# Moving PSUM copies, turns and a value product in the first batch of a fused attention and MLP kernel

## The chip, the cores and the metric

The kernel runs on one core of a Trainium2 chip. A core has a matrix engine (TensorE, in the profile PE, with its weight loads as PEld), a vector engine (VectorE, DVE), a scalar engine (ScalarE, ACT), a general engine (GpSimd, POOL) and an engine that only issues transfers (SyncE, SP). Each has its own queue of instructions, and they are tied together by semaphores. TensorE writes into PSUM; DVE and ACT copy from there into SBUF, the working memory.

The metric is the device time of one launch in microseconds (us), smaller is better. Of several runs the median is given. A profile is one more execution, recorded instruction by instruction; "span" is the time from its first to its last instruction.

## The reference

Two things are computed one after the other: an attention in which scores far below a row's maximum are dropped, and a two-layer MLP with an exact GELU. Cut to what matters:

```python
batch, n_heads, seq, head_dim = (8, 8, 576, 64)
scores = q @ k^T / sqrt(head_dim)
thresh = max(scores, axis=-1) - tau
scores = where(scores >= thresh, scores, -1e9)
attn   = exp(scores - max(scores)); attn /= sum(attn) + 1e-9
x = (attn @ v) transposed and reshaped to (4608, 512)
h = x @ w_in                      # 512 x 2048
g = 0.5 * h * (1 + erf(h / sqrt(2)))
out = g @ w_out                   # 2048 x 512
```

All inputs and the result are float32; the weights w_in and w_out arrive in a wider type and are converted in the kernel.

## The kernel before, in words

**Tiles.** Two heads are handled as a pair p (32 pairs; 4 of them make one batch element). A pair's 576 query rows are cut into five chunks i: four of 128 and a last one (i == NC, NC = 4) that holds the 64 remaining rows of both heads. One chunk of one pair is a "slot" n. The loop over slots (L1130) writes out, slot by slot, what every engine does; the order in which an engine gets its instructions is the order of these calls. Nothing is scheduled behind the program's back (`manual_schedule`).

**A slot.** `scores` (L392) multiplies q and k on PE into two PSUM tiles `sc` of two banks each (one tile for the last chunk); there are only two such tiles in all. `softmax_head` (L404) takes row maxima on DVE (L413), thresholds on POOL (L416) and exp on ACT (L418). `softmax_tail` (L421) applies the threshold and sums on DVE (L434), and only then are the score banks free for the next slot.

**The first batch.** The first four pairs (`EARLY`, slots 0 to 19, `BATCH` = 20) are worked in two rounds: chunks 0 and 1 of all four pairs (slots 0 to 7), then chunks 2, 3 and 4 (slots 8 to 19). Their probabilities p are turned by TensorE: `turn_p_early` (L337) turns 128x128 pieces into PSUM tiles named `tr`, and copies them into `pT` (L354, L363 for a full chunk; L358, L367 for the last one, on ACT, but on DVE for the last pair). A slot's turns are called in the next slot. `weigh_v` (L557) multiplies v with pT on PE (L572) into one PSUM tile `xT` and copies x^T into `xall` (L582, ACT). The tiles `tr`, `xT`, `hT`, `o_ps` and `idle` share four PSUM banks (tag "mm"). From slot 20 on (pairs 4 to 31) p is turned on DVE instead (L533) and regrouped by transfers that SP issues (L555).

**Which x^T when.** A list `due` holds what the next slot shall weigh. The second part of a pair's rows (columns TOK = 256 to S = 576) is entered one slot after the pair's last chunk has been turned: the x^T of pairs 0, 1, 2 is weighed in slots 12, 15, 18 and that of pair 3 in slot 21.

**Conversions.** The weights come as 64-bit words. `convert_first` (L188) does two ACT instructions (L199, L200) for a piece, `convert_second` (L203) two on DVE (L207, L208), and `add_low_bits` one on POOL (L219) a slot later. In slots 12, 15 and 18, before x^T is weighed, `convert_ahead` puts several pieces' ACT parts into ACT's queue.

**The MLP.** `fill` (L688) puts matmuls of the MLP between a slot's scores and the next: first layer hT (L664), second layer o_ps (L679). How many is set by `goal`, a table of how much should be done by slot n; `owed` is what is still to be put in. In the first batch the first layer of block 0 is done and its results are held without GELU (L631); in slot 20, `gelus_held` (L641) applies the eight GELUs in one go, between two loads of ACT's function table. Slot 20 puts in no MLP work; slot 21 puts in a share of 0.4 of what is owed, and slot 22 the rest.

**Keeping TensorE busy.** `keep_busy` (L292) puts dummy matmuls of the identity matrix into the queue at the end of the slots that `BUSY` (L1123) lists; slot 20 has eight.

Of the kernel before, what the change touches and what calls it, by code (L numbers as in the profile page):

```python
# [18 lines left out]
def kernel(  # L19
# [28 lines left out]
    nc = tc.nc  # L48
    ctx.enter_context(tc.manual_schedule())

    B, H, S, D = q.shape
    d_model, d_ff = moe_w_in.shape
    P = 128
    Q = 32
    HP = H // 2
    NP = B * HP
    EARLY = HP
    NC = S // P
    MAIN = NC * P
    TAIL = S - MAIN  # L60
# [5 lines left out]
    TOK = 256  # L66
# [89 lines left out]
    LATER = 2  # L156
# [65 lines left out]
    def convert_ahead(steps):  # L222

        while raws and len(ahead) <= steps:
            convert_first()
# [111 lines left out]
    def turn_p_early(p, i):  # L337


        s = st[p]  # L340
        if i == 0 or (p < HP and i == 2):
            s["pT"] = [one.tile([P, KR, S], FP32, tag=f"pT{e}", name=f"pT{e}") for e in range(2)]
        w = s.pop(("p", i))
        n = 1 if i == NC else 2

        def turn(to, at):
            nc.tensor.transpose(to, w[:, at:at + P], ident)  # L347

        for e in range(n):
            tr = ps.tile([P, NC, P], FP32, tag="mm", name="tr")  # L350
            for c in range(NC):
                turn(tr[:, c, :], e * (S + TAIL) + c * P)
            if i < NC:
                nc.scalar.copy(s["pT"][e][:, 0:NC, i * P:(i + 1) * P], tr)  # L354
        if i == NC:
            copy = nc.vector.tensor_copy if p == EARLY - 1 else nc.scalar.copy
            for e in range(2):
                copy(s["pT"][e][:, 0:NC, MAIN:S], tr[:, :, e * TAIL:(e + 1) * TAIL])  # L358
        tails = s["pT"][0][:, NC, :]
        tr = ps.tile([P, NC, P], FP32, tag="mm", name="tr")  # L360
        turn(tr[:, 0, :], MAIN if i < NC else S - P)
        if i < NC:
            nc.scalar.copy(tails[:, i * P:(i + 1) * P], tr[:, 0, :])  # L363
            return
        for e in range(2):
            rows = slice(e * TAIL, (e + 1) * TAIL)
            copy(tails[rows, MAIN:S], tr[P - TAIL:P, 0, rows])  # L367

    def scale_q(p):
        t = st[p]["q"]  # L370
# [183 lines left out]
            for e in (1, 0):  # L554
                nc.sync.dma_start(by_64(s["pT"][e])[:, 2 * a + h, :, :], turned_p[rows, e, h, :, :])  # L555

    def weigh_v(p, lo, hi):  # L557


        b, hp = divmod(p, HP)  # L560
        s = st[p]
        xT = ps.tile([P, 512], FP32, tag="mm", name="xT")
        for c in range(KR):
            for e in range(2):
                f = slice(e * D, (e + 1) * D)
                to = xT[f, 0:hi - lo]
                if p < EARLY:
                    rhs = s["pT"][0 if c == NC else e][:, c, lo:hi]
                else:
                    to = to.rearrange("p (g s) -> p g s", s=2 * Q)  # L570
                    rhs = by_64(s["pT"][e])[:, lo // (2 * Q):hi // (2 * Q), c, :]
                nc.tensor.matmul(  # L572
                    to, lhsT=s["v"][:, e, c, :], rhs=rhs, start=(c == 0), stop=(c == KR - 1))
        for n, o, at, size in in_blocks(b, lo, hi):
            if n not in x_blk:
                x_at[n] = x_slot(x_place(n))
                x_blk[n] = xall[:, x_at[n], :, :]
            to, x = x_blk[n][:, hp, o:o + size], xT[:, at - lo:at - lo + size]
            if p < EARLY and size == TOK:
                to = to.rearrange("q (p c) -> q c p", c=2)  # L580
                x = x.rearrange("q (c p) -> q c p", c=2)
            nc.scalar.copy(to, x)  # L582

    def weigh_half(p, c):

# [14 lines left out]
    def in_blocks(b, lo, hi):  # L600
        while lo < hi:
            n, o = divmod(b * S + lo, TOK)
            size = min(TOK - o, hi - lo)
            yield n, o, lo, size
            lo += size
# [495 lines left out]
    BATCH = HP * SLOTS  # L1101
# [3 lines left out]
    START = 2 * HP + 2  # L1105
# [14 lines left out]
    HALVED = (2, 3)  # L1120
    DIVIDE_LATE = {14: 0, 16: 1, 19: 2, 22: 3}
    STEPS = [0, 1, 1, 1, 1, 1, 2, 1, 2, 2, 2, 2, 3, 2, 2, 3, 2, 2, 2]
    BUSY = {1: 2, 6: 2, 8: 2, BATCH: 4}  # L1123

    tokens = 0
    owed = 0.0
    due = []
    leaving = []
    loads = iter(())
    for n in range(len(slots) + WEIGH + 1):  # L1130
        p, i = slots[n] if n < len(slots) else divmod(n, SLOTS)
        early = p < EARLY
        last = slots[n - 1] if 0 < n <= len(slots) else None
        if p < NP:
            scores(p, i)
            softmax_head(p, i)
            add_low_bits()
            if last and last[0] < EARLY and last[1] < 2:
                invert(*last)
            if last and last[0] < EARLY and last[1] == NC:  # L1140
                divisors_early(last[0])
            if p < HP - 1 and i == 0:
                turn_qk_early(p + 1)
        elif n == len(slots):
            early_end.close()
            weights_first()
        gelus(0)
        if n == BATCH:
            gelus_held()
        table()  # L1150
        if early and n > START and any(hi == S for _, *_, hi in due):
            convert_ahead(STEPS[n] if n < BATCH - 1 else LATER)
        for args in due:
            if len(args) == 2:
                weigh_half(*args)
                if args[1]:
                    divide_early(args[0], 0, TOK)
                continue
            weigh_v(*args)
            if args[1] == 0:  # L1160
                divide_early(*args)
        due = []
        if n in DIVIDE_LATE:
            divide_late(DIVIDE_LATE[n])
        if p > EARLY and i == WEIGH:
            for lo, hi in (0, WIDE), (WIDE, S):
                weigh_v(p - 1, lo, hi)
            if p == NP:
                divide(p - 1)
        owed += (goal(n) - goal(n - 1)) * BLK_NS * (PARTS[i] if not early and p < NP else 1.0)  # L1170
        if early:
            fill(owed, tokens)
            owed = 0.0
            table()
        if last and last[0] < EARLY and last[1] < NC:
            turn_p_early(*last)
        if p < NP:
            softmax_tail(p, i)
        if p < NP and not early:
            turn_p(p, i)  # L1180
        if p < NP and not early:
            if i == 2:
                regroup(p, 1)
            if i > 2:
                regroup(p, i)
            if i == NC:
                divisors(p)
        if last and last[0] < EARLY and last[1] == NC:
            turn_p_early(*last)
        if p < 2 and i == 0:  # L1190
            for _ in range(2):
                load_piece()
            load_v_early(p + 2)
        if n == START + 1:
            loads = load_steps(HP)
            next(loads)
            next(loads)
        if n == START + 3:
            for _ in loads:
                pass  # L1200
        if n == BATCH - 3:
            load(HP + 1)
        if n == BATCH:
            for t in pd_tail + [turned_p[:, e, h, :, :] for e in range(2) for h in range(2)]:
                nc.gpsimd.memset(t[:, NB:4 * KR, :], 0.0)
        if EARLY < p < NP and i == DIVIDE:
            divide(p - 1)
        if p >= HP and i == 1 and p + 2 < NP:
            loads = load_steps(p + 2)
        if p >= HP:  # L1210
            next(loads, None)
        if p >= HP and i == 1 and p + 1 < NP or p == HP - 1 and i == 2:
            scale_q(p + 1)
        if p >= HP - 1 and i == 2 and p + 1 < NP:
            turn_qk(p + 1)
        convert(STEPS[n] if n < BATCH - 1 else len(pieces))
        if not early:
            lag[0] = 2 if p < NP else 0
            if n != BATCH:
                share = 0.4 if n == BATCH + 1 else 1.0  # L1220
                fill(owed * share, tokens)
                owed *= 1.0 - share
        if n in BUSY:
            keep_busy(BUSY[n])
        if last and last[0] < EARLY:
            if last[1] < 2 and last[0] in HALVED:
                due.append((last[0], last[1]))
            elif last[1] == 1:
                due.append((last[0], 0, TOK))
            if last[1] == NC:  # L1230
                due.append((last[0], TOK, S))
        if n == START - 1:
            tokens = TOK
        elif n == BATCH + 1:
            tokens = S
        elif p > EARLY and i == DIVIDE and p % HP == 0 or p == NP and i == WEIGH:
            tokens = p // HP * S
            leaving += [n for n in AWAY if n in x_blk and (n + 1) * TOK <= tokens]
        elif leaving and i < 2:
            put_away(leaving.pop(0))  # L1240
# [35 lines left out]
```

## Time and profile before

| what | us |
|---|---|
| median of 3 runs | 1333.94 (1333.72 to 1334.61) |
| the profiled execution | 1333.98 |
| its span | 1332.1 |
| PE busy | 1317.4 (99%) |
| DVE busy | 1041.0 (78%) |
| ACT busy | 603.8 (45%) |
| POOL busy | 635.2 (48%) |

Slots have no name in the profile; they are found by the starts of their scores (L401): slot 12 at 69.27 us, 13 at 79.08, 14 at 84.18, 15 at 89.00, 16 at 98.87, 17 at 103.97, 18 at 109.04, 19 at 118.97, 20 at 123.61, 21 at 127.52, 22 at 136.69, 23 at 144.43, 24 at 150.00 and 25 at 153.63.

In the timelines a line gives start and duration in us, the engine, the source line, the operation, what it writes and reads, and how many were merged; in brackets stands how long the engine sat idle just before and what released it. A float32 matmul is recorded as two matmuls, so "x8" is four products. In the view of waits a line names who waited for whom, the total in us, how often, and the longest.

### The profile page before, as it was taken

How to read it: one execution, taken by the hardware profiler on the slowest of the kernel's cores; microseconds unless marked ns; L12 is line 12 of the kernel's file. 1: busy time of each engine (PE TensorE's matmuls, PEld its weight loads, DVE VectorE, ACT ScalarE, POOL GpSimd, SP SyncE). 2: the span in 40 equal slices, each digit the busy share in tenths (PEclk: the TensorE clock that was granted, in tenths of full speed). 3: DMA queues.
4: the chain of work that ended last, by engine and by line, in shares of the span. 5: the costliest groups of instructions: out<-in, count | busy, mean ns of one | idle time of the engine just before them, and what ended most of it. 6: DMA issues, size and time to landing. Idle time of an engine off the chain costs nothing.

```text
span 1332.1 us, 19898 instructions
## 1 busy us (share of the span) xinstructions
PE 1317.4 (99%) x6322; PEld 891.8 (67%) x6322; DVE 1041.0 (78%) x2003; ACT 603.8 (45%) x1025; POOL 635.2 (48%) x1058
## 2 busy tenths in 40 slices
PE   9999999999999999999999999999999999999998
PEld 6766466476476466466466556568788787877877
DVE  6887787788888888888888888783857698386674
ACT  7987357267367358348448438232211203211120
POOL 3555454545655655655655641236264403645530
PEclk9999999999999999999999999999999999999999
DMA  8463666776876887887797775400000130000003
GB/s 257 167 180 86 135 149 155 167 171 154 188 176 153 191 191 156 188 201 160 181 211 155 174 180 113 107 8 1 1 0 1 40 103 17 0 1 0 1 0 79
DMA packets 213687, 153.14 MB, mean 115 GB/s; under 512 B 117264, under 2 KB 196992, under 8 KB 213584
## 3 DMA queue, kind: packets, MB, share of 16 engines
q1 hardware_dynamic: 195440, 125.31, 40.6%
q0 software_dynamic: 17712, 26.26, 7.6%
q8 instruction: 52, 0.85, 0.3%
q14 instruction: 51, 0.42, 0.1%
q10 hardware_dynamic: 432, 0.30, 0.1%
HBM read 56.62 MB, written 12.58 MB: 52 GB/s over the span
## 4 chain that ended last, share of the span: by engine, by line
PE 91%; DVE 3%; ACT 2%; issue 1%; DMA 1%; POOL 1%; SPq 0%; DVEq 0%; POOLq 0%; ACTq 0%
PE bank L852 34%; PE o_ps L679 17%; PE hT L664 16%; PE sc L401 13%; PE xT L572 11%; DVE nmx L413 1%; DVE p L434 1%; ACT p L418 1%; PE tr L347 1%; DVE power L208 1%; DVE power L207 1%; ACT power L199 0%; DMA inv<-turned 0%; ACT w_out L200 0%; POOL thr L416 0%
## 5 line engine op out<-in xcount | busy, mean ns | idle before, releaser
L418 ACT ACTIVATE p<-sc,nmx 128x576 f32<-128x576 f32 x288 | 201.8, 737 | 282.3 <-DVE nmx L413 282.0
L434 DVE SCALAR_TENSOR_TENSOR p<-sc,thr,p 128x576 f32<-128x576 f32 x288 | 225.2, 815 | 72.9 <-ACT p L418 65.2
L416 POOL TENSOR_SCALAR thr<-nmx,tau_eff 128x1 f32<-128x1 f32 x288 | 83.9, 293 | 342.7 <-DVE nmx L413 340.8
L413 DVE TENSOR_REDUCE nmx<-sc 128x1 f32<-128x576 f32 x288 | 205.3, 749 | 46.9 <-PE sc L401 45.6
L664 PE MATMUL hT<-xall,w_in 128*128 128x256 f32 x1024 | 241.8, 386 | 0.0
L679 PE MATMUL o_ps<-w_out,g 128*128 128x512 f32 x512 | 236.8, 603 | 0.0
L664 PEld LDWEIGHTS hT<-xall,w_in 128*128 128x128 f32 x1024 | 189.4, 190 | 51.2 <-issue 24.5
L734 DVE TENSOR_TENSOR o<-o,bank 128x256 f32<-128x256 f32 (+1 forms) x242 | 99.9, 416 | 94.6 <-PE bank L852 89.6
L734 DVE TENSOR_TENSOR c<-c,bank 128x320 f32<-128x320 f32 x304 | 147.1, 487 | 33.8 <-PE bank L852 20.1
L679 PEld LDWEIGHTS o_ps<-w_out,g 128*128 128x128 f32 x512 | 93.1, 190 | 109.6 <-issue 106.5
L401 PE MATMUL sc<-kT,qT 64*128 64x288 f32 x960 | 159.8, 429 | 2.3 <-DVE p L434 1.6
L572 PE MATMUL xT<-pT,v 128*64 128x320 f32 (+1 forms) x1240 | 159.6, 409 | 0.7 <-DVE pT L358 0.5
L533 DVE STREAM_TRANSPOSE turned_p<-p 128x1152 f32<-128x1152 f32 x112 | 154.4, 1378 | 3.9
L401 PEld LDWEIGHTS sc<-kT,qT 64*128 64x128 f32 x960 | 91.4, 186 | 75.8 <-issue 60.4
L572 PEld LDWEIGHTS xT<-pT,v 128*64 128x64 f32 x1240 | 86.5, 137 | 71.5 <-issue 11.1
L852 PE MATMUL bank<-w_out,c 128*128 128x256 f32 (+1 forms) x484 | 120.5, 379 | 0.8 <-DVE o L734 0.8
L260 POOL DMA_DIRECT2D v<-in_v_dram x208 | 110.8, 536 | 3.7 <-issue 1.7
L852 PEld LDWEIGHTS bank<-w_out,c 128*128 128x128 f32 x484 | 90.3, 190 | 18.9 <-DVE o L734 3.2
L919 ACT ACTIVATE c<-c 128x320 f32<-128x320 f32 (+1 forms) x80 | 46.9, 624 | 114.6 <-DVE c L734 114.5
L852 PE MATMUL bank<-t_out,g 128*128 128x256 f32 (+1 forms) x324 | 82.4, 377 | 0.4 <-DVE o L734 0.4
L852 PE MATMUL bank<-t_out,c 128*128 128x256 f32 x320 | 82.8, 381 | 0.0
L734 POOL TENSOR_TENSOR c<-c,g 128x320 f32<-128x320 f32 (+1 forms) x40 | 50.5, 1271 | 67.5 <-DVE c L734 67.5
(186 smaller groups left out, 1753.7 us busy)
## 6 DMA issues: line engine op xcount, KB each, us to landing
pT<-turned_p SPq DMA_DIRECT2D x448, 160.0 KB, 3.6
pT<-pd_tail SPq DMA_DIRECT2D x112, 80.0 KB, 3.1
q<-in_q_dram POOLq DMA_DIRECT2D x104, 72.0 KB, 3.6
k<-in_k_dram POOLq DMA_DIRECT2D x104, 72.0 KB, 3.2
inv<-turned SPq DMA_DIRECT2D x54, 128.0 KB, 4.2
v<-in_v_dram POOLq DMA_DIRECT2D x156, 40.0 KB, 3.2
out_dram<-o SPq DMA_DIRECT2D x40, 128.0 KB, 2.4
xall<-in_moe_w_out_dram SPq DMA_DIRECT2D x9, 512.0 KB, 5.0
```

What stands on the lines that cost most here:

```text
L260: eng.dma_start(t[r:P:4, e, 0:n, :], rows[:, r * KR:r * KR + n, :])
L401: nc.tensor.matmul(sc[e][:, h, 0:HALF], lhsT=lhsT, rhs=s["kT"][rows, at:at + HALF], start=True, stop=True)
L413: nc.vector.tensor_reduce(nmx[:, e:e + 1], sc, axis=AXIS.XY, op=ALU.max, negate=True)
L416: nc.gpsimd.tensor_scalar(thr[:, e:e + 1], nmx[:, e:e + 1], -1.0, tau_eff, op0=ALU.mult, op1=ALU.subtract)
L418: nc.scalar.activation(w[:, e * S:(e + 1) * S].rearrange("p (h s) -> p h s", h=2), sc, AF.Exp, bias=nmx[:, e:e + 1], scale=1.0)
L434: nc.vector.scalar_tensor_tensor(row, sc[e][:, :, 0:HALF], thr[:, e:e + 1], row, op0=ALU.is_ge, op1=ALU.mult, accum_out=den[e])
L533: nc.vector.transpose(turned_p[:, :, i // 2, 0:NB, i % 2 * Q:(i % 2 + 1) * Q], w.rearrange("p (e b i) -> p e b i", e=2, i=Q))
L572: nc.tensor.matmul(to, lhsT=s["v"][:, e, c, :], rhs=rhs, start=(c == 0), stop=(c == KR - 1))
L664: nc.tensor.matmul(hT[:, j % 2, :], lhsT=w_in_sb[c][:, j * P:(j + 1) * P], rhs=x_blk[n][:, c, :], start=(c == 0), stop=(c == N_DM - 1))
L679: nc.tensor.matmul(o[:, 0:d_model], lhsT=g[j][:, m * P:(m + 1) * P], rhs=w_out_sb[j], start=(j == 0), stop=(j == N_DF - 1))
L734: eng.tensor_tensor(out, a, b, op=ALU.add)
L852: nc.tensor.matmul(to, lhsT=l, rhs=r, start=start and k == 0, stop=k == len(pairs) - 1, skip_group_check=not start)
```

## The change

Four edits, all around the first batch:

- In slots 12, 15 and 18, `convert_ahead` is called after the x^T of that slot has been weighed and its copies are in ACT's queue, no longer before.
- The last chunk of pair 3 (slot 19) is turned at the end of slot 19 instead of in slot 20, and its four copies into pT are done by ACT instead of DVE.
- The second x^T of pair 3 is weighed in slot 20, right behind that slot's scores, instead of in slot 21; its copies (new function `weighed`) are done by DVE, behind slot 20's `turn_p`.
- Slot 21 gets a share of 0.75 of the owed MLP work instead of 0.4 (eight products of the second layer instead of four; slot 22 gets three instead of seven), and the eight dummy products of slot 20 are dropped.

```diff
         if i == NC:
-            copy = nc.vector.tensor_copy if p == EARLY - 1 else nc.scalar.copy
             for e in range(2):
-                copy(s["pT"][e][:, 0:NC, MAIN:S], tr[:, :, e * TAIL:(e + 1) * TAIL])
+                nc.scalar.copy(s["pT"][e][:, 0:NC, MAIN:S], tr[:, :, e * TAIL:(e + 1) * TAIL])
...
-            copy(tails[rows, MAIN:S], tr[P - TAIL:P, 0, rows])
+            nc.scalar.copy(tails[rows, MAIN:S], tr[P - TAIL:P, 0, rows])
...
-    def weigh_v(p, lo, hi):
+    def weigh_v(p, lo, hi, copy=nc.scalar.copy):
...
+        if copy is None:
+            return xT
+        weighed(p, lo, hi, xT, copy)
+
+    def weighed(p, lo, hi, xT, copy):
+
+
+        b, hp = divmod(p, HP)
         for n, o, at, size in in_blocks(b, lo, hi):
...
-            nc.scalar.copy(to, x)
+            copy(to, x)
...
-    BUSY = {1: 2, 6: 2, 8: 2, BATCH: 4}
+    BUSY = {1: 2, 6: 2, 8: 2}
...
-        if early and n > START and any(hi == S for _, *_, hi in due):
-            convert_ahead(STEPS[n] if n < BATCH - 1 else LATER)
+        long = early and n > START and any(hi == S for _, *_, hi in due)
         for args in due:
...
+            if n == BATCH:
+                xT = weigh_v(*args, None)
+                continue
             weigh_v(*args)
             if args[1] == 0:
                 divide_early(*args)
         due = []
+        if long:
+            convert_ahead(STEPS[n] if n < BATCH - 1 else LATER)
...
         if p < NP:
             softmax_tail(p, i)
+        if n == BATCH - 1:
+            turn_p_early(p, i)
         if p < NP and not early:
             turn_p(p, i)
+        if n == BATCH:
+            weighed(EARLY - 1, TOK, S, xT, nc.vector.tensor_copy)
...
-        if last and last[0] < EARLY and last[1] == NC:
+        if last and last[0] < EARLY and last[1] == NC and early:
             turn_p_early(*last)
...
-                share = 0.4 if n == BATCH + 1 else 1.0
+                share = 0.75 if n == BATCH + 1 else 1.0
...
-            if last[1] == NC:
+            if last[1] == NC and early:
                 due.append((last[0], TOK, S))
+            if n == BATCH - 1:
+                due.append((p, TOK, S))
```

## The prediction

> **What bounds the kernel now.** I read the page's busy table and its chain first, then what TensorE (PE) waited for between 60 and 165 us, then the timelines of PE, VectorE (DVE) and ScalarE (ACT) there.
>
> ```profile
> PE 1317.4 (99%) x6322; PEld 891.8 (67%) x6322; DVE 1041.0 (78%) x2003; ACT 603.8 (45%) x1025; POOL 635.2 (48%) x1058
> PE 91%; DVE 3%; ACT 2%; issue 1%; DMA 1%; POOL 1%; SPq 0%; DVEq 0%; POOLq 0%; ACTq 0%
> ...
> PE tr L347 <- ACT xall L582: 2.4, 3, 0.9
> PE sc L401 <- DVE p L434: 0.9, 3, 0.5
> PE xT L572 <- DVE pT L358: 0.5, 1, 0.5
> ```
>
> PE carries the end: from 150 us on it waits 1.5 us in all, so what PE gains before 155 us arrives at the end undiminished. The second block shows what there is to gain: three waits of the turns for x^T's copies (slots 12, 15, 18), and small ones around slot 21. PE's timeline has them in place (the three pairs of turns are slots 12, 15 and 18; the rest is slots 20 to 23):
>
> ```profile
> 77.11 0.60 PE L347 MATMUL tr<-ident,p 128*128 128x128 f32 x4
> 78.44 0.81 PE L347 MATMUL tr<-ident,p 128*128 128x128 f32 x5 [0.72 <-ACT xall L582]
> ...
> 96.85 1.04 PE L347 MATMUL tr<-ident,p 128*128 128x128 f32 x8
> 98.71 0.33 PE L347 MATMUL tr<-ident,p 128*128 128x128 f32 x1 [0.83 <-ACT xall L582]
> ...
> 116.78 0.66 PE L347 MATMUL tr<-ident,p 128*128 128x128 f32 x4 [0.31 <-ACT g L631]
> 118.31 0.82 PE L347 MATMUL tr<-ident,p 128*128 128x128 f32 x5 [0.88 <-ACT xall L582]
> ...
> 125.38 1.95 PE L297 MATMUL idle<-ident 128*128 128x128 f32 x16
> 127.52 1.94 PE L401 MATMUL sc<-kT,qT 64*128 64x288 f32 x8 [0.19 <-DVE p L434]
> 129.98 3.14 PE L572 MATMUL xT<-pT,v 128*64 128x320 f32 x20 [0.52 <-DVE pT L358]
> 133.06 3.70 PE L679 MATMUL o_ps<-w_out,g 128*128 128x512 f32 x8
> 136.69 1.61 PE L401 MATMUL sc<-kT,qT 64*128 64x288 f32 x8
> ```
>
> The 16 dummy records and the waits beside them are PE time without use. DVE's timeline says how much faster the softmax could go there; its reductions of slots 23, 24 and 25:
>
> ```profile
> 145.70 1.42 DVE L413 TENSOR_REDUCE nmx<-sc 128x1 f32<-128x576 f32 x2 [1.23 <-PE sc L401]
> 151.17 0.76 DVE L413 TENSOR_REDUCE nmx<-sc 128x1 f32<-128x576 f32 x1 [0.86 <-PE sc L401]
> 154.91 1.42 DVE L413 TENSOR_REDUCE nmx<-sc 128x1 f32<-128x576 f32 x2
> ```
>
> **What the Trainium skill says.** "PSUM — Partial Sum Buffer", section "Engine vs sequencer instructions": the queues of ACT, DVE and POOL are strictly first in, first out, and matmuls start in program order. The trace agrees: the copy L582 stands at 77.92 us behind 3.46 us of conversions (74.46 to 77.92), though x^T had ended by 73.99. "Perfetto Trace Analysis", "Tensor Engine Instruction": a matmul's end is estimated, so I count from start to start. "TensorE: Matmul & The Clock Gate", "What's actually happening": the clock halves after about 3.4 us without work; the windows show a clock of 1.00 throughout, and the longest PE gap that I get below is 0.9 us, so dropping the dummies should cost nothing there. "SBUF — State Buffer", "Who interferes with whom": a DVE instruction with two SBUF inputs and a POOL instruction that reads SBUF lock each other out; L208 takes 0.69 us mostly but 1.64 at 83.08 and 102.88, both times beside POOL's L219, which agrees.
>
> **Part 1, conversions behind the copies (slots 12, 15, 18).** ACT does the same work in another order, so what follows both (the copies L354 of the turns) starts where it did; only the x^T bank is free sooner, by 3.46, 3.46 and 1.14 us. What is late next? A slot turns into three PSUM tiles, A (4 turns), B (4) and C (1). In slot 15 only C waits for x^T's bank, A and B ran at once (x8). There C follows B at once and the next scores start after nine turns, 1.08 us (122.53 to 123.61 in slot 19), so at 97.93 instead of 98.87: 0.94 us. In slots 12 and 18 it is B that waits, and C, in the program as built, takes the bank of A and waits for A's copy L354. That copy stays behind the conversions: slot 12, start 78.28, and C about 0.64 later (as 83.28 to 83.92 in slot 13), 78.92; before, B from 78.44 plus four turns of 0.117 gave 78.91. Gain 0. Slot 18: copy at 118.12, C at 118.76, scores at 118.92 instead of 118.97: 0.05. So of the 2.4 us that the waits view shows, most only changes its name to "tr waits for pT L354". I take 0.97 us: 0.94 + 0 + 0.05, less 0.02 for POOL (below). Bounds: 0.05, if slot 15's gain is lost too, and 2.9, if C were free in all three (0.89 + 0.94 + 1.07).
>
> Does slot 15's 0.94 reach slot 20? The next exp waited 1.05 us for its maximum, so ACT can give it. POOL's L219 at 98.89 to 100.16 doesn't move and holds the threshold L416 to 100.18 instead of 100.04; the threshold of slot 17, behind POOL's L219 and L478, is then 0.80 earlier instead of 0.94, but slot 18's DVE chain waits for ACT's L371, which has the full 0.94. The conversions themselves come 0.36 us later; DVE's L207 takes those of the turn before, POOL's sums are due a slot later: no cost.
>
> **Part 2, slots 19 to 25.** Times here are in the frame of before, part 1 left out.
> - The last five turns move ahead of slot 20's scores. PE ends slot 19's nine at 123.61; A' needs A's copy (123.17 + 0.64 = 123.81), four turns 0.47, then C' after B's copy (124.24) at 124.29, and from C to scores 0.27 (103.71 to 103.97): 124.56 instead of 123.61. **Slot 20 is 0.95 later**, and all that hangs on it.
> - Their copies L358 and L367 go from DVE (1.2 us) to ACT (1.08), at 124.4 to 125.5, into ACT's wait of 1.26 for exp: free; without that wait they would cost 1.08.
> - The 8 dummies (1.95 us) go, x^T follows the scores at 125.7 with its operands there, 2.85 us to 128.6; slot 21's scores to 129.9.
> - ACT's held GELUs: exp, copy, table, first GELU are one queue from 125.67 on, so 0.95 later: first result about 130.4. PE waits 0.6 there, then eight o_ps of 0.907 (four took 3.63) to 137.7.
> - exp of slot 21 is behind the GELUs: 135.50 instead of 134.55. x^T's copy on DVE (about 0.6, an estimate from L358's 0.39 for 256 columns, bounds 0.4 and 0.8) lies before slot 21's reduction, after which DVE waited 3.26: free.
> - From here DVE sets the pace. PE has three o_ps in slot 22 (2.72) instead of seven and is ready for slot 23's scores at 141.9, but their second bank is free only when L434 of slot 22 ends, 142.4. Slot 23's reduction stands behind two transposes and turn_qk, at 144.48 + 0.95 = 145.43 instead of 145.70; slot 24's behind L533, 150.0 instead of 151.17. In one line: DVE had 1.23 + 0.86 = 2.09 us of waits to give, less 0.95 for the late start, **1.14 us**; PE's scores of slot 25 wait for L434 of slot 24 in both and gain the same. After it DVE waits about 1 us per slot again and PE leads.
> - No DMA is added. SP's regrouping starts behind L533 of slot 21, 0.95 later (138.51); its last issue then ends at 162.0, lands 3.1 later, and x^T wants it at about 168: 3 us to spare. POOL's issues keep their place.
>
> **Sum.** 0.97 + 1.14 = 2.1 us. The profiled execution took 1333.98 us (span 1332.1 and 1.9 around it), so 1331.9; the median of the runs is 0.04 lower, so **1331.8**. What a measurement of this kernel can tell from no change is about 0.2%, 2.7 us: the forecast is just inside.
>
> **Rivals.**
> - All three waits vanish (C isn't held in slots 12 and 18): 0.89 + 1.02 more, 1329.9. For it: the waits view blames L582 alone. Against: C's bank.
> - DVE doesn't bind in slots 22 to 25, PE does. From 124.56: scores 1.17, x^T 2.85, scores, 0.6 of wait, eight o_ps, scores 1.17, three o_ps, scores, five o_ps (4.40), scores 0.97, three (2.66), scores end at 151.9 instead of 154.91: 3.0 instead of 1.14, 1330.0. Against: slot 25's reduction shows no wait at all before.
> - Both: 1328.1.
> - No change: a restart of PE after each wait costs more than I read, or part 1 gives nothing: 1333 to 1334.4.
> - Slower: the port lock. POOL's sums L219 and DVE's L207 and L208 are moved against each other in slots 12 to 20; each further collision costs 0.95 us (1.64 less 0.69), and slots 14, 17 and 18 start their reductions straight behind these instructions. Between two and three more eat the gain, from the sixth on it is slower by 0.2%, and six give 1337.5. Against: most of the two queues shifts together.
>
> **Chances.** Forecast (1331.2 to 1332.6) 0.42, a quarter of it beyond 0.2%; all three waits 0.10; PE binds 0.16; both 0.05; no change 0.14; slower 0.13. So faster 0.42, same 0.45, slower 0.13. The range 1329.4 to 1334.4 leaves out both-at-once and slower, 0.18.
>
> **What would show it.** Right: the wait "tr for xall L582" gone, "tr for pT L354" grown to about 2 us, with slot 12's next scores no earlier; slot 15's 0.9 us earlier; no dummies in slot 20; a wait of o_ps for the first GELU of about 0.6 us; DVE without a wait before slot 24's reduction. Wrong: C free in slots 12 and 18, a PE clock under 1.00, L208 rows of 1.64 us in new places, or PE gaps after 165 us.

## The result

The changed kernel takes 1331.51 us in the median of 15 runs (1330.61 to 1332.61), the kernel before 1333.95 on the same chip (15 runs, 1332.53 to 1334.94). The ratio is 0.9981, with a 95% interval from 0.9974 to 0.9989. The change is 2.4 us faster; 1331.8 had been predicted. The profiled execution took 1331.37 us, with a span of 1329.2.

The starts of the scores are a sharper measure than the medians, since they leave out what happens before and after the edited stretch. From the start of slot 12's scores to the start of slot 26's (L401 of before, L400 of after) it takes 90.13 us before and 88.02 after: 2.11 less, against 2.11 in the prediction (0.97 + 1.14). The rest of the 2.9 us between the two spans is not the change's: slot 12 already starts 0.32 earlier, before any edited instruction, and at about 590 and 690 us the lead grew by 0.2 and 0.5 in this pair of profiles. The same places shift by such amounts, up or down, in the profiles below. So all kernels are compared by these 90 us, with the medians beside them. A ratio can differ in its last digit from the quotient of the two medians.

### The profile after

Line numbers have moved: L582 is now L589, L401 is L400, L413 is L412, L434 is L433, L572 is L571, L679 is L686. The busy table and the chain of the page of after:

```profile
PE 1315.9 (99%) x6306; PEld 891.0 (67%) x6306; DVE 1040.7 (78%) x2001; ACT 604.3 (45%) x1027; POOL 635.2 (48%) x1058
PE 93%; DVE 3%; ACT 2%; issue 1%; DMA 0%; POOL 0%; DVEq 0%; ACTq 0%; POOLq 0%
```

PE lost 16 records (the eight dummies), and on balance two copies went from DVE to ACT (four into pT to ACT, two of x^T to DVE). What PE waited for between 60 and 165 us (who for whom, total in us, times, longest):

```profile
PE tr L347 <- ACT pT L354: 2.2, 4, 0.9
PE sc L400 <- DVE p L433: 0.7, 2, 0.5
PE tr L347 <- ACT g L638: 0.3, 1, 0.3
PE o_ps L686 <- ACT g L644: 0.2, 1, 0.2
```

The wait of the turns for x^T's copies (2.4 us before) is gone, and a wait for A's copy L354 has grown from 0.5 to 2.2. Read alone, this view says that part 1 brought 0.7 us. PE's timeline of after says where it brought something (slots 12, 15 and 18, then 20 to 25):

```profile
76.79 1.03 PE L347 MATMUL tr<-ident,p 128*128 128x128 f32 x8
78.60 0.33 PE L347 MATMUL tr<-ident,p 128*128 128x128 f32 x1 [0.77 <-ACT pT L354]
...
96.55 1.15 PE L347 MATMUL tr<-ident,p 128*128 128x128 f32 x9
97.53 1.14 PE L400 MATMUL sc<-pd_tail,q_tail 128*128 128x288 f32 x4
...
117.58 0.33 PE L347 MATMUL tr<-ident,p 128*128 128x128 f32 x1 [0.91 <-ACT pT L354]
...
124.51 2.91 PE L571 MATMUL xT<-pT,v 128*64 128x320 f32 x20
127.35 1.84 PE L400 MATMUL sc<-kT,qT 64*128 64x288 f32 x8
129.37 7.11 PE L686 MATMUL o_ps<-w_out,g 128*128 128x512 f32 x16 [0.17 <-ACT g L644]
136.41 1.62 PE L400 MATMUL sc<-kT,qT 64*128 64x288 f32 x8
...
140.72 1.79 PE L400 MATMUL sc<-kT,qT 64*128 64x288 f32 x8
...
150.56 1.99 PE L400 MATMUL sc<-kT,qT 64*128 64x288 f32 x8
```

In slots 12 and 18, B now runs with A (x8) and C waits in B's stead. Only in slot 15 do all nine turns run in one go. In slots 20 to 25 PE has no long gap left, but the scores of slots 21, 22, 23 and 25 take 1.62 to 1.99 us where 1.24 is the work: short pauses inside them, for banks. DVE's timeline of after, the reductions of slots 23, 24 and 25:

```profile
144.24 1.42 DVE L412 TENSOR_REDUCE nmx<-sc 128x1 f32<-128x576 f32 x2
148.77 0.72 DVE L412 TENSOR_REDUCE nmx<-sc 128x1 f32<-128x576 f32 x1
152.48 1.38 DVE L412 TENSOR_REDUCE nmx<-sc 128x1 f32<-128x576 f32 x2
```

The waits of 1.23 and 0.86 us that two of them had are gone: DVE runs through.

Us from one slot's scores to the next, for the slots that an edit moves, and the sum over slots 12 to 25 (the other slots are the same within 0.05 us in these four):

| slot | before | after | part 1 alone | part 2 alone |
|---|---|---|---|---|
| 12 | 9.81 | 9.82 | 9.82 | 9.83 |
| 15 | 9.87 | 8.82 | 8.82 | 9.86 |
| 16 | 5.10 | 5.24 | 5.21 | 5.10 |
| 18 | 9.93 | 9.93 | 9.91 | 9.94 |
| 19 | 4.64 | 5.59 | 4.63 | 5.59 |
| 20 | 3.91 | 4.01 | 3.92 | 4.01 |
| 21 | 9.17 | 9.06 | 9.17 | 9.05 |
| 22 | 7.74 | 4.31 | 7.74 | 4.32 |
| 23 | 5.57 | 6.12 | 5.57 | 6.12 |
| 24 | 3.63 | 3.72 | 3.64 | 3.72 |
| 25 | 5.77 | 6.41 | 5.76 | 6.40 |
| 12 to 25 | 90.13 | 88.02 | 89.21 | 88.95 |

### The profile page after: what moved, and what is told of

The parts are those of the page before. It is cut to its first block, busy times and chain, and to the rows that moved or that the text cites. A ratio compares the mean times of both kernels' runs of the same rounds, so it can differ in the third digit from the quotient of the medians.

```text
span 1329.2 us, 19865 instructions
## 1 busy us (share of the span) xinstructions
PE 1315.9 (99%) x6306; PEld 891.0 (67%) x6306; DVE 1040.7 (78%) x2001; ACT 604.3 (45%) x1027; POOL 635.2 (48%) x1058
## 4 chain that ended last, share of the span: by engine, by line
PE 93%; DVE 3%; ACT 2%; issue 1%; DMA 0%; POOL 0%; DVEq 0%; ACTq 0%; POOLq 0%
PE bank L859 34%; PE o_ps L686 17%; PE hT L671 16%; PE sc L400 13%; PE xT L571 11%; DVE nmx L412 1%; ACT p L417 1%; DVE power L208 1%; DVE p L433 1%; DVE power L207 1%; PE tr L347 1%; DMA q<-in_q_dram 0%; ACT pT L354 0%; PE tr L317 0%; PE idle L147 0%
## 5 line engine op out<-in xcount | busy, mean ns | idle before, releaser
L433 DVE SCALAR_TENSOR_TENSOR p<-sc,thr,p 128x576 f32<-128x576 f32 x288 | 225.3, 816 | 72.6 <-ACT p L417 66.1
L412 DVE TENSOR_REDUCE nmx<-sc 128x1 f32<-128x576 f32 x288 | 205.4, 750 | 44.9 <-PE sc L400 43.7
L686 PE MATMUL o_ps<-w_out,g 128*128 128x512 f32 x512 | 236.8, 603 | 0.2 <-ACT g L644 0.2
L686 PEld LDWEIGHTS o_ps<-w_out,g 128*128 128x128 f32 x512 | 93.2, 190 | 109.5 <-issue 106.7
L400 PE MATMUL sc<-kT,qT 64*128 64x288 f32 x960 | 160.5, 429 | 1.9 <-DVE p L433 1.2
L571 PE MATMUL xT<-pT,v 128*64 128x320 f32 (+1 forms) x1240 | 159.4, 410 | 0.2
L400 PEld LDWEIGHTS sc<-kT,qT 64*128 64x128 f32 x960 | 91.9, 186 | 75.8 <-issue 60.8
L571 PEld LDWEIGHTS xT<-pT,v 128*64 128x64 f32 x1240 | 86.4, 137 | 70.8 <-issue 11.1
```

What stands on the lines that cost most here:

```text
L400: nc.tensor.matmul(sc[e][:, h, 0:HALF], lhsT=lhsT, rhs=s["kT"][rows, at:at + HALF], start=True, stop=True)
L412: nc.vector.tensor_reduce(nmx[:, e:e + 1], sc, axis=AXIS.XY, op=ALU.max, negate=True)
L433: nc.vector.scalar_tensor_tensor(row, sc[e][:, :, 0:HALF], thr[:, e:e + 1], row, op0=ALU.is_ge, op1=ALU.mult, accum_out=den[e])
L571: nc.tensor.matmul(to, lhsT=s["v"][:, e, c, :], rhs=rhs, start=(c == 0), stop=(c == KR - 1))
L686: nc.tensor.matmul(o[:, 0:d_model], lhsT=g[j][:, m * P:(m + 1) * P], rhs=w_out_sb[j], start=(j == 0), stop=(j == N_DF - 1))
```

## The experiments

The theory: part 1 brings something in slot 15 only, because C is held by A's copy in slots 12 and 18; part 2 brings what DVE had in waits, less the late start of slot 20. The rivals: all three waits vanish, or PE and not DVE sets the pace from slot 22 on. Ten kernels were run; all medians are over at least 6 runs, beside runs of the kernel before on the same chip. An edit is shown against the changed kernel, with three exceptions: part 1 alone and the two runs with fewer dummies are shown against the kernel before, the dummies in the pause against the run ahead of them, and the version with both findings without the part that stands under pair 5.

### Part 1 alone

```diff
-        if early and n > START and any(hi == S for _, *_, hi in due):
-            convert_ahead(STEPS[n] if n < BATCH - 1 else LATER)
+        long = early and n > START and any(hi == S for _, *_, hi in due)
...
         due = []
+        if long:
+            convert_ahead(STEPS[n] if n < BATCH - 1 else LATER)
```

> Part 1 alone (the kernel before, with the conversions of slots 12, 15 and 18 behind x^T's copies). My theory: 0.97 us less than before, all of it in slot 15, where only the single last turn C waits: scores 15 to scores 16 takes 8.9 instead of 9.87 us, while slot 12 stays at 9.8 and slot 18 at 9.9 us because C there waits for A's copy L354 behind the conversions. Rival (the three waits are what the waits view says, all three vanish): 2.9 us less, slots 12, 15 and 18 each about 0.9 us shorter. In slots 20 to 25 nothing changes in either: dummies stay, and DVE keeps its waits of 1.23 and 0.86 us before the reductions of slots 23 and 24.

Measured: 1332.88 us, ratio 0.9994 (0.9985 to 1.0002), which does not tell it from no change. The slots do: 0.92 us less, all of it in slot 15 (1.05, of which slot 16 gives 0.11 back), nothing in slots 12 and 18. The rival's 2.9 us are out. PE's timeline of this kernel in slot 12 shows the same C as in after:

```profile
76.68 1.04 PE L347 MATMUL tr<-ident,p 128*128 128x128 f32 x8
78.49 0.33 PE L347 MATMUL tr<-ident,p 128*128 128x128 f32 x1 [0.77 <-ACT pT L354]
```

### Part 2 alone

```diff
         long = early and n > START and any(hi == S for _, *_, hi in due)
+        if long:
+            convert_ahead(STEPS[n] if n < BATCH - 1 else LATER)
...
         due = []
-        if long:
-            convert_ahead(STEPS[n] if n < BATCH - 1 else LATER)
```

> Part 2 alone (the changed kernel, with the conversions of slots 12, 15 and 18 back ahead of x^T). My theory (DVE sets the pace from slot 22 on): 1.14 us less than before, 0.97 more than the changed kernel; slot 20's scores 0.95 later than before, and slot 26's about 1.1 to 1.2 earlier; slots 12, 15 and 18 as before. Rival (PE sets the pace): 3.0 us less than before. If the parts don't add (part 2 absorbs what part 1 gives) the sum of both runs' gains is over the 2.44 us of the whole change.

Measured: 1332.68 us, ratio 0.9991 (0.9983 to 0.9999), and 1.18 us less by the slots; 1.14 was predicted. The parts add: 0.92 + 1.18 = 2.10 against 2.11 for both. DVE's timeline of this kernel, the reductions of slots 23 and 24, can be laid beside the prediction's times (145.43 and 150.0):

```profile
145.40 1.42 DVE L412 TENSOR_REDUCE nmx<-sc 128x1 f32<-128x576 f32 x2
149.93 0.72 DVE L412 TENSOR_REDUCE nmx<-sc 128x1 f32<-128x576 f32 x1
```

### Conversions behind the copies of the turns

```diff
-        if long:
+        if long and n == 15:
             convert_ahead(STEPS[n] if n < BATCH - 1 else LATER)
...
             turn_p_early(*last)
+        if long and n != 15:
+            convert_ahead(STEPS[n] if n < BATCH - 1 else LATER)
```

> The changed kernel, with the conversions of slots 12 and 18 (not 15) also behind the copies L354 and L362 of the slot's turns. If A's copy is what holds C there: C follows B at once, slot 12's length falls from 9.8 to 8.9 us and slot 18's from 9.9 to 8.9, together 1.9. The price: slot 12's conversions (3.46 us) now end at about 82.1 and slot 13's exp and L638 start 1.4 us later, so the copies of slot 13's turns and its own C come about 0.4 later. Sum about 1.5 us less than the changed kernel. Rival (ACT's chain binds, its work only moves): 0, slots 13 and 19 longer by what 12 and 18 lose. If C waits for something else: lengths unchanged.

Measured: 1333.74 us, ratio 0.9996 (0.9988 to 1.0004); by the slots 90.55 us, 2.5 more than the changed kernel. What holds C was named rightly: with A's copy no longer behind the conversions its wait falls to 0.29 us in both slots, and slots 12 and 18 are 0.48 and 0.63 shorter (9.34 and 9.30). Not 0.9 each, because the copy itself still has to run beside B's turns. The price was missed by far: slots 13, 14 and 15 grew by 0.98, 1.10 and 1.69. For slots 13 and 14, DVE's timeline of this kernel, conversions and the reduction from slot 12 to slot 13, shows where it begins:

```profile
79.66 0.43 DVE L207 TENSOR_SCALAR power<-power 128x512 uint32<-128x512 uint32 x1 [3.34 <-ACT power L199]
80.12 0.69 DVE L208 SCALAR_TENSOR_TENSOR power<-turned_p,power 128x512 uint32<-128x512 uint32 x1
80.80 0.43 DVE L207 TENSOR_SCALAR power<-power 128x512 uint32<-128x512 uint32 x1
81.27 0.69 DVE L208 SCALAR_TENSOR_TENSOR power<-xall,power 128x512 uint32<-128x512 uint32 x1
81.87 0.75 DVE L412 TENSOR_REDUCE nmx<-sc 128x1 f32<-128x576 f32 x1
```

DVE's part of two of the conversions is queued in slot 12. Now it waits 3.34 us for ACT's part, and the reduction of slot 13 stands behind it: it starts at 81.87, where the scores, begun at 78.59, would have let it start at about 79.8 (in after they begin at 78.77 and it starts at 79.94). The delay is handed on: slot 15's scores wait 1.36 us for slot 14's L433. I had looked at ACT's queue for the price and forgotten DVE's. In the change itself the conversions move by 0.36 us only, and DVE does not notice.

Slot 15's 1.69 us have another cause, TensorE's clock. PE's timeline and the windows of this kernel (in a window: stretch in us, its length, PE busy and records, granted clock, DMA share, GB/s):

```profile
90.61 1.94 PE L400 MATMUL sc<-pd_tail,qT 64*128 64x288 f32 x8 [1.36 <-DVE p L433]
92.48 4.60 PE L571 MATMUL xT<-pT,v 128*64 128x320 f32 x20
```

```profile
89.11:92.53 3.42, 2.05 (x12) 1.00 0.22 61
92.53:95.94 3.41, 3.41 (x15) 0.50 0.64 186
95.94:99.36 3.42, 3.42 (x19) 1.00 0.38 147
```

After a pause of 1.36 us the clock was 0.50 for 3.41 us, and x^T took 4.53 us from its start to the first hT, where it takes 2.84 in after: 1.69 more, all that slot 15 lost. Without it this kernel would be 0.84 us behind the changed one, an estimate (90.55 less 1.69 less 88.02). Nor does it happen in every execution: five of the 13 runs took 1331.33 to 1332.23 us, and eight, the profiled one among them, 1333.36 to 1334.65. What decides is taken up below, after the run with half of the dummies.

### Pair 5's q and k turned earlier

```diff
+        if n == BATCH + 1:
+            turn_qk(HP + 1)
         if p < NP:
             softmax_tail(p, i)
         if n == BATCH - 1:
             turn_p_early(p, i)
+            scale_q(HP + 1)
...
-        if p >= HP and i == 1 and p + 1 < NP or p == HP - 1 and i == 2:
+        if p > HP and i == 1 and p + 1 < NP or p == HP - 1 and i == 2:
...
-        if p >= HP - 1 and i == 2 and p + 1 < NP:
+        if p >= HP - 1 and i == 2 and p + 1 < NP and p != HP:
```

> The changed kernel, with the turning of pair 5's q and k (L382, L383, L388, 1.74 us of DVE in slot 22) moved ahead into DVE's wait of 4.1 us for slot 21's exp, and the scaling of that q (L370, 0.77 us of ACT) moved into ACT's wait before slot 20's exp. PE's work is the same. If DVE sets the pace in slots 22 to 25: slot 23's reduction up to 1.74 us earlier. PE then limits: of its pauses only the 0.75 us within slot 25's scores (1.99 instead of 1.24 us) goes, the 0.55 within slot 23's stays, since that waits for slot 22's L433, which doesn't move. So 0.75 us less than the changed kernel. Rivals: DVE alone counts, 1.7 us less; PE alone counts, nothing.

Measured: 1330.36 us, ratio 0.9974 to the kernel before (0.9965 to 0.9984); by the slots 87.26 us, 0.76 less than the changed kernel. PE's work is the same and only the order on DVE and ACT differs. ACT's move (the scaling of q) brings nothing of its own that shows: slot 22's first L433, which waits for ACT's exp, starts 0.18 us earlier than in after, and slot 22's scores 0.19. So DVE did hold slots 23 to 25. DVE's timeline of this kernel, the reductions of slots 23, 24 and 25:

```profile
142.32 1.38 DVE L412 TENSOR_REDUCE nmx<-sc 128x1 f32<-128x576 f32 x2
...
147.83 0.76 DVE L412 TENSOR_REDUCE nmx<-sc 128x1 f32<-128x576 f32 x1 [0.94 <-PE sc L400]
...
151.58 1.41 DVE L412 TENSOR_REDUCE nmx<-sc 128x1 f32<-128x576 f32 x2
```

Slot 23's starts 1.92 us earlier than in after (0.19 of it was there already at slot 22's scores), then DVE waits 0.94 us for PE: from there PE has the lead. Slots 22 and 23 keep their length (4.32 and 6.12), slot 25 falls from 6.41 to 5.77, because its scores no longer pause for slot 24's L433.

### Slot 21's share back at 0.4

```diff
-                share = 0.75 if n == BATCH + 1 else 1.0
+                share = 0.4 if n == BATCH + 1 else 1.0
```

> The changed kernel with slot 21's share of the owed MLP work back at 0.4 (four o_ps in slot 21, seven in slot 22). With four o_ps PE reaches slot 22's scores at about 133.0, but their banks come free only with slot 21's two L433 (ended at 135.9 and 136.7 behind the exp that follows the GELUs): about 3 us of PE time without work. DVE has its own slack at first, then slot 24's seven-plus-five o_ps arrive late: slot 26's scores about 1.75 us later than in the changed kernel. Rival (DVE sets the pace, the split of PE's work makes no difference): 0.

Measured: 1336.78 us, ratio 1.0021 (1.0014 to 1.0027): slower than the kernel before. By the slots 92.94 us, 4.92 more than the changed kernel, where I had expected 1.75. The pause came as expected, 3.04 us, but what follows it is too long. PE's timeline and the windows of this kernel:

```profile
128.96 3.67 PE L686 MATMUL o_ps<-w_out,g 128*128 128x512 f32 x8 [0.17 <-ACT g L644]
135.67 2.99 PE L400 MATMUL sc<-kT,qT 64*128 64x288 f32 x8 [3.04 <-DVE p L433]
138.59 7.97 PE L686 MATMUL o_ps<-w_out,g 128*128 128x512 f32 x14
```

```profile
131.80:135.21 3.41, 0.83 (x2) 1.00 0.37 90
135.21:138.62 3.41, 2.95 (x9) 0.50 0.00 0
138.62:142.04 3.42, 3.42 (x5) 0.50 0.78 154
142.04:145.45 3.41, 3.41 (x9) 1.00 0.94 206
```

The granted clock was 0.50 for 6.83 us, from just before the end of the pause on. The seven o_ps took 7.97 us, where the kernel before takes 6.28 for as many.

### The same, with dummies in the pause

```diff
-    BUSY = {1: 2, 6: 2, 8: 2}
+    BUSY = {1: 2, 6: 2, 8: 2, BATCH + 1: 6}
```

> The changed kernel with slot 21's share at 0.4, as in the run before, and twelve dummy products (2.9 us of PE) behind slot 21's four o_ps, where PE paused 3.04 us for slot 21's L433 and the windows then showed a clock of 0.5 for some 7 us. If the clock fell because of the pause: it stays at 1.00, slot 22's scores start at the same place, its seven o_ps take 6.35 instead of 7.97 us, and from slot 12 to slot 26 the scores take about 90.0 us (88.0 in the changed kernel, 92.9 in the run before), the 2 us above the changed kernel being what the order of the work costs. Rival (the clock has another cause): 92.9 as before, or more.

Measured: 1333.69 us, ratio 1.0001 (0.9993 to 1.0010), and 90.15 us by the slots; 90.0 was expected. The clock is 1.00 throughout and the seven o_ps take 6.28 us. Of the 4.92 us that the smaller share cost, 2.8 were the clock and 2.1 the order of the work. Where the 2.1 lie, DVE's timeline of this kernel shows (slots 23 and 24):

```profile
144.93 1.42 DVE L412 TENSOR_REDUCE nmx<-sc 128x1 f32<-128x576 f32 x2 [1.22 <-PE sc L400]
150.39 0.76 DVE L412 TENSOR_REDUCE nmx<-sc 128x1 f32<-128x576 f32 x1 [0.85 <-PE sc L400]
```

These are the kernel before's waits of 1.23 and 0.86 us, back again, 2.07 in sum. So it is the share that takes them out. And against part 1 alone, which has these waits too (89.21 us), this kernel is 0.94 slower: the size of slot 20's late start.

### The dummies put back into the changed kernel

```diff
-    BUSY = {1: 2, 6: 2, 8: 2}
+    BUSY = {1: 2, 6: 2, 8: 2, BATCH: 4}
```

> The changed kernel with the eight dummy products of slot 20 put back (1.95 us of PE, behind x^T, ahead of slot 21's scores). Theory: about 0.9 us slower than the changed kernel: 0.65 of it fits into PE's wait for the first GELU, 0.4 into the pause within slot 22's scores, which then reach DVE's reduction of slot 22 about 0.9 us late, and DVE passes that on to slot 26. Rival (PE sets the pace): 1.95 slower. Rival (they are filler without a price, also here): 0.

Measured: 1332.78 us, ratio to the kernel before 0.9994 (0.9986 to 1.0002); 88.88 us by the slots, 0.86 more than the changed kernel. Of the 1.95 us, over half disappears into pauses that were there anyway, and the rest reaches DVE. Its reduction of slot 22 waits 0.75 us for PE, where it waited for nothing in after:

```profile
138.54 1.42 DVE L412 TENSOR_REDUCE nmx<-sc 128x1 f32<-128x576 f32 x2 [0.75 <-PE sc L400]
```

### The kernel before without the dummies, and with half of them

```diff
-    BUSY = {1: 2, 6: 2, 8: 2, BATCH: 4}
+    BUSY = {1: 2, 6: 2, 8: 2}
```

> The kernel before with nothing changed but the eight dummies of slot 20 dropped. Theory: no gain (0 to 0.2 us), since slot 21's scores wait there for slot 20's L434 (ended at 127.5), which doesn't move: the wait of 0.19 us grows to about 2.1, the clock stays at 1.00. Rival: 1.95 us faster, if the dummies are PE time lost.

Measured: 1334.86 us against 1333.68, ratio 1.0008 (0.9999 to 1.0016). By the slots 91.31 us, 1.18 more than before: not the nothing that I expected, and far from the rival's gain. PE's timeline and the windows of this kernel:

```profile
127.50 1.94 PE L401 MATMUL sc<-kT,qT 64*128 64x288 f32 x8 [1.98 <-DVE p L434]
129.96 4.64 PE L572 MATMUL xT<-pT,v 128*64 128x320 f32 x20 [0.52 <-DVE pT L358]
```

```profile
126.42:129.84 3.42, 1.93 (x8) 1.00 0.05 8
129.84:133.25 3.41, 3.29 (x13) 0.50 0.21 45
133.25:136.66 3.41, 3.41 (x15) 1.00 0.36 87
```

The pause of 1.98 us is followed, 2.34 us after its end, by 3.41 us at half clock, just when x^T runs: 4.57 us from its start to the first o_ps, where it took 3.08 with the dummies.

With half of them:

```diff
-    BUSY = {1: 2, 6: 2, 8: 2, BATCH: 4}
+    BUSY = {1: 2, 6: 2, 8: 2, BATCH: 2}
```

> The kernel before with four of slot 20's eight dummy products left (0.98 us). With none PE paused 1.98 us there and the clock was 0.5 from about 129.8 to 132.8 us, which cost 1.2 us (slot 12 to slot 26). Theory: a pause of about 1.2 us (then a stretch of scores that wait, 1.94 us for 1.2 us of work, and 0.52 for the copies) is short enough, the clock stays at 1.00 and the time is that of the kernel before: 90.1 us from slot 12 to 26. Rival (any pause of over 1 us, or the sum of the pauses, lowers it): between 90.4 and 91.3.

Measured: 1333.64 us, ratio 1.0002 (0.9994 to 1.0010), and in the profiled execution 90.18 us by the slots, as before. PE's timeline of that execution has a pause of 1.08 us and x^T at its usual speed:

```profile
126.82 1.94 PE L401 MATMUL sc<-kT,qT 64*128 64x288 f32 x8 [1.08 <-DVE p L434]
129.28 3.15 PE L572 MATMUL xT<-pT,v 128*64 128x320 f32 x20 [0.52 <-DVE pT L358]
```

But four of the 13 runs took 1335.47 to 1335.68 us, with a granted clock of 0.998, and the other nine 1332.64 to 1334.35, with 0.999. So the pause is short enough in most executions, not in all, and the rival is not out.

**When the clock falls.** Three profiles have such a fall: the conversions behind the turns' copies, the share of 0.4, and the kernel before without dummies. The low stretches last 3.41, 6.83 and 3.41 us, and from the end of each to the next fall, behind the last products, lie 362, 349 and 351 times 3.413 us. So the clock changes on a grid of 3.413 us, whose place differs from profile to profile. In the window of the grid just ahead of the fall, PE was idle for 0.40, 0.76 and 0.44 of the time (busy 2.05, 0.83 and 1.93 us). The most idle window with no fall behind it (114.73 to 118.14 us with the share of 0.4, busy 2.22 us) has 0.35. So the pauses of one window count together, and here the border lies between 0.35 and 0.40. This is inferred from these traces, in which the ends of products are modelled; why the clock stayed low for two windows with the share of 0.4 is open.

This would explain the four runs. With half of the dummies the profile's window over the pauses (124.50 to 127.91 us, busy 2.31) is idle for 0.32; laid from 125.74 to 129.15 it would be idle for 0.44 (busy 1.93). The table gives, as an estimate from each trace, in what share of all places of the grid some window is idle for over 0.38, and beside it the runs with a clock of 0.998 or less or a fall in the profile. Most of these runs were not traced, so for them the cause is argued, not shown.

| kernel | share of places, estimate | runs with a lower clock |
|---|---|---|
| share 0.4 | 1.00 | 20 of 20 |
| before without dummies | 0.98 | 13 of 13 |
| conversions behind the turns' copies | 0.64 | 8 of 13 |
| before with half of them | 0.15 | 4 of 13 |
| all others | 0 (idle 0.36 at most) | none |

### A version with both findings

Pair 5's turning early, as above, and part of the conversions behind the turns' copies: in slot 12 only the last piece, which DVE takes a slot later anyway, in slot 18 all.

```diff
-        if long:
-            convert_ahead(STEPS[n] if n < BATCH - 1 else LATER)
+        if long and n < 18:
+            convert_ahead(STEPS[n] - (n == 12))
...
             turn_p_early(*last)
+        if long and n in (12, 18):
+            convert_ahead(STEPS[n])
```

> The changed kernel with pair 5's turning moved early as in the run before (0.76 us by the starts of the scores), and in slots 12 and 18 a part of the conversions behind the copies of the turns: in slot 12 only the last piece (two ACT instructions, 1.15 us, which DVE takes a slot later anyway), in slot 18 all (two instructions). C then waits for A's copy alone: slot 12 0.48 us shorter, slot 18 0.63, as measured with all conversions behind the copies, without the late DVE of slots 13 to 15. Together 1.1 us less than pair 5's turning alone, 1.9 less than the changed kernel. Rival (DVE starves as it did there): slots 13 to 15 longer by 1 us or more, no gain.

Measured: 1329.97 us, ratio to the kernel before 0.9971 (0.9960 to 0.9983), which beats both kernels. By the slots 86.17 us, 1.09 less than with pair 5's turning alone and 1.85 less than the changed kernel; slots 12 and 18 take 9.34 and 9.23 us, slots 13 to 15 stay as in after. The medians of the two differ by 0.39 only: in the profiles its lead over the other shrinks by 0.6 after slot 28, where nothing differs between them, and the spread of the runs does not allow more to be said. PE's timeline of this kernel in slot 12:

```profile
76.61 1.04 PE L347 MATMUL tr<-ident,p 128*128 128x128 f32 x8
77.94 0.33 PE L347 MATMUL tr<-ident,p 128*128 128x128 f32 x1 [0.29 <-ACT pT L354]
```

All kernels in one table (a positive difference is slower than before):

| kernel | slots 12 to 25, us | minus before | median minus before |
|---|---|---|---|
| the change | 88.02 | -2.11 | -2.44 |
| part 1 alone | 89.21 | -0.92 | -0.75 |
| part 2 alone | 88.95 | -1.18 | -0.95 |
| conversions behind the turns' copies | 90.55 | +0.42 | +0.11 |
| pair 5 turned early | 87.26 | -2.87 | -3.27 |
| share 0.4 | 92.94 | +2.81 | +3.10 |
| share 0.4, dummies in the pause | 90.15 | +0.02 | -0.05 |
| dummies put back | 88.88 | -1.25 | -0.90 |
| before without dummies | 91.31 | +1.18 | +1.18 |
| before with half of them | 90.18 | +0.05 | -0.10 |
| both findings | 86.17 | -3.96 | -3.71 |

The two columns agree within 0.4 us; the intervals of the ratios are wider, about 1.1 us to each side. The medians of the conversions behind the copies and of half of the dummies are taken over two groups of runs each, as told above.

## Why the prediction was right

**Part 1: right, slot by slot.** Predicted 0.94, 0 and 0.05 us for slots 15, 12 and 18, less 0.02; measured with part 1 alone 1.05, -0.01 and 0.02, less 0.11 in slot 16. The prediction's 0.02 was a wait for POOL; this is another one. In after, hT's six products there take 2.73 us from their start to the first turn, 2.59 before: they start at 98.50, while ACT still copies slot 15's turns (L354, 98.27 to 99.40), and a weight load of hT waits 0.3 us for L354 (0.2 in part 1 alone), which before does not show. With 0.01 or 0.02 in some other slots the sum is 0.92 instead of 0.97. The reason, A's copy L354 behind the conversions, is shown by taking the conversions out of its way, not only by the name in the waits view: C's wait fell to 0.29 us.

**The start of slot 20: right.** Predicted 0.95 us later, measured 0.95 (slot 19 takes 5.59 instead of 4.64).

**The wait for the first GELU: right in kind, its size only bounded.** Predicted 0.6 us. From the scores' start to the first o_ps it is 2.02 us; less 1.17 for the scores, 0.85 is left. Part of that are the scores' own pauses for a bank (they are recorded as 1.84 us where 1.24 is the work), so what belongs to the GELU alone lies between the bracket's 0.17 and 0.85.

**DVE sets the pace: right, with a limit.** Predicted 2.09 us of waits less 0.95, 1.14; measured 1.18. Both terms can be seen apart: with the smaller share and the clock held, the waits come back (1.22 and 0.85). That DVE and not PE held slots 23 to 25 follows from pair 5's early turning, which gave 0.76 us. The rival's estimate, 3.0 us if PE alone mattered, was not reached even then (1.18 + 0.76 = 1.94): scores of slot 23 still pause for slot 22's L433, which hangs on ACT's GELUs.

**The dummies: the one step that was wrong.** The prediction called the dummies "PE time without use" in the kernel before. They were not: without them that kernel loses 1.18 us to a lowered clock. For the changed kernel the step held, because x^T stands where the dummies stood: in its trace no stretch of 3.41 us between 119 and 150 us, wherever it is laid, has PE idle for more than 0.05 of it. So the number did not suffer. What failed is the bound behind it. "TensorE: Matmul & The Clock Gate", section "What's actually happening", gives an idle window of about 3.4 us; here windows of 3.41 us in which PE was idle for 0.40 to 0.76 of the time were enough for a clock of 0.5, with longest pauses of 1.36, 1.98 and 3.04 us. My expectations for the smaller share (1.75, measured 4.92) and for the kernel before without dummies (0, measured 1.18) failed for this reason, and with the conversions behind the copies it made 1.69 us of the miss.

**The slower rival, the port lock, did not happen.** L208 takes 1.65 us at 82.78 and 1.64 at 101.67 in after, in slots 13 and 16, where before has its two (83.08 and 102.88).

## What to carry to other kernels

When a wait is removed, look up which buffer the next instruction takes and what it waits for: of three waits of equal size in the waits view one was worth 1 us and two nothing, and the difference was the rotation of the banks and one copy's place in a queue. Before work is moved later on one engine, look at the other engine that has its second half in queue: it waits in order, and everything behind it waits too. Work that seems to fill PE's time for nothing may keep its clock up; if it is taken out, put useful work in the same place, as this change does with x^T. And one profile does not show that a pause is harmless: with half of the dummies it shows a full clock, while four of 13 runs were about 2 us longer.

## What the runs showed of the hardware

- TensorE's clock fell to 0.50 for 3.41 us (twice 3.41 in one profile) after a window of 3.41 us in which PE was idle for 0.40, 0.44 or 0.76 of the time, and stayed at 1.00 after one with 0.35. The longest pauses were 1.36, 1.98 and 3.04 us. With a longest pause of 1.08 us it stayed at 1.00 in the profile, but four of 13 runs had a lower mean clock and took about 2 us longer.
- Twelve dummy products in the pause of 3.04 us, of which 0.36 was left, kept the clock at 1.00.
- The low clock can fall on work that has nothing to do with the pause: after the pause of 1.98 us it began 2.34 us after PE was back at work, so that it fell on x^T. After the pause of 3.04 us it was there when PE resumed.
